# Attention and two feed-forward stages on one core: the turned one-hot evicted by VectorE, parameter blocks in odd steps, dummies among similarities, two casts moved

## The chip, the core and the metric

The kernel runs on one core of a Trainium2 chip. The metric is the device time of one execution in microseconds (us). Before the change the median of three runs is 686.15 us (684.75 to 687.68).

## What is computed

Clustered attention (two batches, 8 heads, 768 tokens, 64 per head), then a feed-forward stage behind a low-rank mixing over tokens, then one with a convolution over tokens and a gate. The change concerns the attention alone:

```python
q_assign = np.argmax(np.einsum('bhsd,hcd->bhsc', q_n, c_n), axis=-1)
k_assign = np.argmax(np.einsum('bhsd,hcd->bhsc', k_n, c_n), axis=-1)
mask = q_assign[:, :, :, None] == k_assign[:, :, None, :]
scores = scale * np.matmul(q, k.transpose(0, 1, 3, 2))
scores = np.where(mask, scores, -1000000000.0)
...
attn = attn / (np.sum(attn, axis=-1, keepdims=True) + 1e-09)
return np.matmul(attn, v).astype(np.float32)
```

## The kernel before

Heads are taken in pairs: 2 batches x 4 pairs, numbered 0 to 7 here. A pair has 12 **steps**, one for each tile of 128 queries of its two heads; 96 steps in all, numbered n, and s is the number of the step in its pair (0 to 11). Python code issues the instructions in the order in which each engine executes them; nothing is rearranged later. The function `step(n)` (L644) issues parts of several tiles:

- TensorE: the scores of tile n + 2 (`s_mm`, L344 from the split operands "ab", L355 from "cd", whose last rows hold the one-hot of the clusters and so the mask), products with v for three finished tiles (`pv_mm`, L406), every third step the turning of the output (`fin_t`, L422), and the transposes of tile n (`t_mm`, L382, two PSUM tiles of three transposes each).
- ScalarE: the rounded half of the transposes of tile n - 1 (`t_hi`, L391), the exponential of tile n + 1 (L373), in steps with s = 0, 3, 6, 9 the copy of the finished product (`fin_a`, L415), in steps 1, 4, 7, 10 that of the turned output (`fin_x`, L428).
- VectorE: the rest of the transposes of tile n - 1 (`t_lo`, L395, which needs L391), and the row maximum of tile n + 2 (`s_max`, L361), written out together with the scaled scores.

The transposes, similarities, turned outputs and turned one-hots share three PSUM tiles (pool `ps_t`, tag "t"): TensorE waits where none of the three has been emptied.

`prep(n)` (L613) issues at the end of a step what the next pair needs. The similarities with the centroids (`sims`, L220, 24 narrow matmuls) run in step 2. VectorE makes a one-hot of them in steps 2 to 5 (L239 to L247), TensorE turns it in step 6 (`onehot_t`, L253), ScalarE evicts it (`onehot_rows`, L259), and SP's queue copies it into "cd" (L267). In pair 0 all of this is one to two steps earlier. POOL splits the next operands (`split_ops`, L130 and L131, issued in steps 1 and 7; `split_v`, L122 and L123, in step 8) and issues their loads (L111 to L113, steps 3 and 10).

The weights arrive as 64-bit numbers and are converted in **parameter blocks**. Seven of them lie under the attention, one behind the other, one a pair: `pump(THIN)` takes the next action of a block at every second step (L642). Before, these are the even steps: DMA in step 2, conversion of the high word on ScalarE (`job_base`, L460) in step 6, the shift of the low word on VectorE (`job_low`, L465) in step 8, the joining of the words (`job_high`, L469) in step 10, the sign (`job_sign`, L473) in step 0 of the next pair, and in step 2 `job_put`: a cast on ScalarE (L519, or L547 for blocks of V; the first block, U, has none) and a subtraction on POOL (L520). From pair 4 on the mixing of batch 0 is issued in steps 0, 8, 9 and 11 as well (L566 to L605), with an addition of 512 columns on VectorE for each tile (L585).

At the start, `first_pair` prepares head 0 on its own; `split_first(1, "q")` (L203 to L205) rounds the second half of head 0's queries with two ScalarE casts and a POOL subtraction, and the loads and splits of head 1 follow on POOL. `warm` (L156) issues dummy matmuls of 384 columns on zeros, whose result is not used. The similarities of pair 1 run at the start too, tiles 0 and 1 before step -2 and tiles 2 to 5 in step 0.

Of the kernel before, what the change touches and what calls it, by code (L numbers as in the profile page):

```python
# [19 lines left out]
AF = mybir.ActivationFunctionType  # L20
ALU = mybir.AluOpType
# [10 lines left out]
def tile_kernel(ctx: ExitStack, tc: tile.TileContext, qk, vv, cen, u_w, v_w, w1, w2, win, wout, conv, out):  # L32
    nc = tc.nc
# [3 lines left out]
    NT = S // P  # L37
# [70 lines left out]
    def load_ops(b, p, j):  # L108
        h = 2 * p + j
        ab, cd = take_ops(b, p, j)  # L110
        nc.gpsimd.dma_start(out=cd[0:D], in_=qk[b, h])  # L111
        nc.gpsimd.dma_start(out=ab[D:2 * D], in_=qk[b, h])
        nc.gpsimd.dma_start(out=ab[0:D, 1 - j], in_=qk[b, h, :, 1 - j])  # L113
# [6 lines left out]
    def split_v(b, p, rv):  # L120
        vt = a_v.tile([P, 2, NT, 2 * D], F32R, tag="vt", name="vt")
        nc.gpsimd.tensor_copy(vt[:, :, :, 0:D], rv)  # L122
        nc.gpsimd.tensor_sub(vt[:, :, :, D:2 * D], rv, vt[:, :, :, 0:D])  # L123
        vts[b, p] = vt

    def split_ops(b, p, j, eng):

        ab, cd = ops[b, 2 * p + j]
        lo, hi = raw[b, p][j], raw[b, p][1 - j]
        eng.tensor_sub(ab[0:D, j], lo[0:D], cd[0:D, j])  # L130
        eng.tensor_sub(ab[D:2 * D, 1 - j], hi[D:2 * D], ab[D:2 * D, 1 - j])  # L131
# [13 lines left out]
    ohs = acon.tile([2 * 2 * NC, 2], F32, name="ohs")  # L145
# [10 lines left out]
    def warm(count):  # L156
        for _ in range(count):
            nc.tensor.matmul(idle, busy[:, 0:P], busy, start=True, stop=True)
# [36 lines left out]
    def split_first(half, which):  # L195
        c = slice(half * HS, (half + 1) * HS)
        if which == "k":
            nc.scalar.copy(cd0[0:D, 1, c], rk0[D:2 * D, c])
            nc.scalar.copy(ab0[0:D, 1, c], rk0[D:2 * D, c])
            nc.gpsimd.tensor_copy(ab0[D:2 * D, 1, c], rk0[D:2 * D, c])  # L200
            nc.vector.tensor_sub(ab0[D:2 * D, 1, c], rk0[D:2 * D, c], ab0[D:2 * D, 1, c])
        else:
            nc.scalar.copy(cd0[0:D, 0, c], rq0[0:D, c])  # L203
            nc.scalar.copy(ab0[D:2 * D, 0, c], rq0[0:D, c])
            nc.gpsimd.tensor_sub(ab0[0:D, 0, c], rq0[0:D, c], cd0[0:D, 0, c])  # L205
# [7 lines left out]
    def sims(b, p, tiles=range(NT)):  # L213
        rq, rk = raw[b, p]
        if (b, p) not in ohst:
            ohst[b, p] = {"pm": ps_t.tile([P, NT * 4, NC], F32, tag="t", name="sim")}
        pm = ohst[b, p]["pm"]
        for t in tiles:
            for i, (r, cb) in enumerate(((rq, cbq), (rk, cbk))):
                nc.tensor.matmul(  # L220
                    pm[:, 4 * t + 2 * i:4 * t + 2 * i + 2, :].rearrange("p g c -> p (g c)"),
                    r[:, t * P:(t + 1) * P], cb[:, p], start=True, stop=True,
                )
# [32 lines left out]
    def onehot_rows(b, p):  # L256
        pt = ohst.pop((b, p))["pt"]
        os_ = a_oh.tile([4 * NC, S], F32R, tag="os", name="os")
        nc.scalar.activation(os_, pt, AF.Identity, scale=ohs[:, 0:1], bias=ohs[:, 1:2])  # L259
        put_rows(b, p, os_, range(2))  # L260

    def put_rows(b, p, os_, heads):
# [104 lines left out]
    def s_exp(n):  # L367
        ps = st.pop(("s", n))
        nb = st.pop(("nb", n))
        if n % 3 == 0:  # L370
            st["sum", n // 3] = a_s.tile([P, 3], F32, tag="sum", name="sum")
        e = st["e", n]
        nc.scalar.activation(e, ps[:, :, 0:HS], AF.Exp, scale=SCALE, bias=nb, accum_out=st["sum", n // 3][:, n % 3:n % 3 + 1])  # L373
# [154 lines left out]
    load_ops(0, 0, 1)  # L528
    rv0 = load_v(0, 0)
    first_pair()  # L530
    split_first(1, "q")
    load_ops(0, 1, 0)
    sims(0, 1, range(2))
    split_ops(0, 0, 1, nc.gpsimd)
    split_v(0, 0, rv0)


    u3 = mixc.tile([P, NT, 3, R], F32, name="u3")
# [74 lines left out]
    def prep(n):  # L613

        pair, s = divmod(n, 2 * NT)
        nxt = pair + 1
        if nxt < B * NP:
            b, p = divmod(nxt, NP)
            for part, at in enumerate((2, 2, 3, 4, 5) if nxt > 1 else (0, 0, 1, 2, 3)):
                if s == at and (nxt > 1 or part > 1):  # L620
                    sims_onehot(b, p, part)
            if s == 1:
                split_ops(b, p, 0, nc.gpsimd)
            elif s == 3:
                load_ops(b, p, 1)
            elif s == 4:
                st["rv"] = load_v(b, p)
            elif s == 7:
                split_ops(b, p, 1, nc.gpsimd)
            elif s == 8:  # L630
                split_v(b, p, st.pop("rv"))
            if s == (6 if nxt > 1 else 5):
                onehot_t(b, p)
                onehot_rows(b, p)
        if s == 10 and pair + 2 < B * NP:
            load_raw(*divmod(pair + 2, NP))
            load_ops(*divmod(pair + 2, NP), 0)
        if n == NQ - 7:
            queue_chunk(1, lambda: wpc)
        if n >= NQ - 7:  # L640
            pump(FLOW)
        elif n % 2 == 0 and n > 0:  # L642
            pump(THIN)

    def step(n):
        pair, s = divmod(n, 2 * NT)
        mix = None
        if s == 8 and pair > 0 and n < NQ:
            b, p = divmod(pair - 1, NP)
            mixing.insert(0, mix_t(b, p))  # L650
            if p == NP - 1:
                mix_rest(b)
        if n == 0:
            sims(0, 1, range(2, NT))
        if n + 2 < NQ:
            s_mm(n + 2)
        g, r = divmod(n - 4, 3)
        if 0 <= g < NHALF:
            pv_mm(g, r)
        if 0 <= g - 1 < NHALF and r == 0:  # L660
            fin_t(g - 1)
        elif mixing and (s in (0, 8, 9, 11) or pair == B * NP - 1):
            mix = mixing.pop(0)
            got = mix[0]()
        if s == 2 and n < NQ and 1 < pair + 1 < B * NP:
            sims(*divmod(pair + 1, NP))
        if 0 <= n < NQ:
            t_mm(n)
        if 0 <= n - 1 < NQ:
            for i in range(2):  # L670
                t_hi(n - 1, i)
                t_lo(n - 1, i)
        if 0 <= n + 1 < NQ:
            s_exp(n + 1)
        if n == 0:
            sims_onehot(0, 1, 0)
            sims_onehot(0, 1, 1)
        if n + 2 < NQ:
            s_max(n + 2)
        if 0 <= g < NHALF and r == 0:  # L680
            sm = st["sum", g]
            nc.gpsimd.tensor_scalar(out=sm, in0=sm, scalar1=1e-9, scalar2=None, op0=ALU.add)
        if 0 <= g < NHALF and r == 2:
            fin_a(g)
        if 0 <= g - 1 < NHALF and r == 0:
            fin_x(g - 1)
        if mix:
            mix[1](got)
        if 0 <= n < NQ:
            prep(n)  # L690

    for n in range(-2, NQ - 2):
        step(n)
# [254 lines left out]
```

## Time and profile before

| | |
|---|---|
| median of three runs | 686.15 us |
| profiled execution, its own time | 687.84 us |
| its span | 685.9 us |
| TensorE busy (matmul) | 666.7 us, 97% |
| VectorE busy | 451.3 us, 66% |
| ScalarE busy | 373.1 us, 54% |
| POOL busy | 292.0 us, 43% |
| mean granted TensorE clock | 0.997 |

Attention takes the first 270 us of the span, up to its last exponential. The shares are averages over the stages: under attention VectorE and ScalarE are busy for 80 to 90% of the time, in the feed-forward stages for much less. Matmuls are pipelined and the ends of their rows are modelled, so TensorE's rate is better read from the starts of its matmuls. In a row of the timeline the engines are PE (TensorE), DVE (VectorE), ACT (ScalarE), POOL (GpSimd) and SPq (SyncE's queue); what stands in brackets is the idle time of the engine before the instruction and what ended it.

### The profile page before, as it was taken

The page shows a single profiled execution, that of the slowest core. Times are in us where ns is not written, and L with a number is a line of the kernel's source. Part 1 is how long each engine was busy: PE and PEld are TensorE (multiplying, and loading weights), DVE is VectorE, ACT ScalarE, POOL GpSimd, SP SyncE. Part 2 cuts the span into 40 slices and gives each one's busy share as a digit, 9 for nine tenths or more (in the row PEclk, how much of TensorE's full clock was granted, in tenths as well). Part 3 has the DMA queues.
Part 4 walks back from the last instruction along what each step waited for, and adds up shares of the span by engine and source line. Part 5 has one row for each costly group of instructions (what it writes and reads, how often), then busy time and mean ns, then how long its engine had stood idle before and what let it go on. Part 6 is the DMA issues. An engine that isn't in the chain of part 4 may idle for free.

```text
span 685.9 us, 10453 instructions
## 1 busy us (share of the span) xinstructions
PE 666.7 (97%) x3782; PEld 586.1 (85%) x3782; DVE 451.3 (66%) x833; ACT 373.1 (54%) x750; POOL 292.0 (43%) x384
## 2 busy tenths in 40 slices
PE   8999999998999999998999999999999999999997
PEld 6899999998899998888888888888887788888886
DVE  6897888888888898668732778775247535543400
ACT  5787787887787898324311443442134357753611
POOL 5775757585657542424530333332024643322300
PEclk9999999999999999999999999999999999999999
DMA  7764545546353501212200444342013000000111
GB/s 181 159 147 78 136 105 123 127 102 146 81 144 86 129 1 32 93 32 93 93 32 3 135 134 127 124 147 70 1 48 133 4 0 1 1 32 16 47 46 47
DMA packets 19587, 55.49 MB, mean 81 GB/s; under 512 B 3312, under 2 KB 7024, under 8 KB 19536
## 3 DMA queue, kind: packets, MB, share of 16 engines
q1 hardware_dynamic: 15936, 40.08, 19.5%
q0 software_dynamic: 3600, 14.75, 10.6%
q8 instruction: 30, 0.49, 0.3%
q14 instruction: 21, 0.17, 0.1%
HBM read 50.19 MB, written 3.15 MB: 78 GB/s over the span
## 4 chain that ended last, share of the span: by engine, by line
PE 78%; DVE 9%; issue 4%; ACT 4%; POOL 3%; DMA 0%; ACTq 0%; POOLq 0%; DVEq 0%
PE g L837 10%; PE tr L382 8%; PE pv L406 7%; PE h L714 5%; PE h L716 5%; PE h L715 5%; PE a L731 5%; PE a L730 5%; PE a L732 5%; PE sc L344 3%; PE sc L355 3%; PE po L871 3%; PE po L872 3%; PE po L873 3%; PE sim L220 2%
## 5 line engine op out<-in xcount | busy, mean ns | idle before, releaser
L520 POOL TENSOR_TENSOR wl<-wx,wh 128x512 fp32r<-128x512 f32 x48 | 63.0, 1314 | 114.9 <-ACT wh L519 114.6
L395 DVE TENSOR_TENSOR pl<-tr,ph 128x384 fp32r<-128x384 f32 x192 | 97.6, 549 | 17.7 <-ACT ph L391 16.9
L391 ACT CAST ph<-tr 128x384 fp32r<-128x384 f32 x192 | 83.8, 485 | 26.4 <-PE tr L382 25.6
L382 PE MATMUL tr<-identf,e 128*128 128x128 f32 x576 | 84.0, 278 | 10.1 <-DVE pl L395 7.5
L361 DVE TENSOR_SCALAR_CACHE_REDUCE e<-sc 128x768 f32<-128x768 f32 x96 | 90.8, 947 | 1.1 <-PE sc L355 1.1
L719 ACT ACTIVATE rh<-h 128x512 fp32r<-128x512 f32 (+1 forms) x52 | 29.3, 563 | 111.8 <-PE h L716 111.8
L373 ACT ACTIVATE e<-sc,nb 128x768 f32<-128x768 f32 x96 | 88.2, 918 | 3.1 <-DVE e L361 3.0
L720 DVE SCALAR_TENSOR_TENSOR rl<-h,rh 128x512 fp32r<-128x512 f32 (+1 forms) x52 | 33.7, 648 | 82.9 <-ACT rh L719 82.8
L382 PEld LDWEIGHTS tr<-identf,e 128*128 128x128 f32 x576 | 66.8, 142 | 19.7 <-DVE pl L395 14.3
L714 PE MATMUL h<-uh,wh 128*128 128x512 f32 (+1 forms) x208 | 78.2, 376 | 1.6 <-DVE rl L720 1.6
L730 PE MATMUL a<-rh,wh 128*128 128x512 f32 (+1 forms) x208 | 78.2, 376 | 0.5 <-DVE xa L746 0.5
L731 PE MATMUL a<-rl,wh 128*128 128x512 f32 (+1 forms) x208 | 77.9, 374 | 0.5 <-DVE rl L720 0.3
L716 PE MATMUL h<-uh,wl 128*128 128x512 f32 (+1 forms) x208 | 77.7, 373 | 0.0
L715 PE MATMUL h<-ul,wh 128*128 128x512 f32 (+1 forms) x208 | 77.7, 373 | 0.0
L732 PE MATMUL a<-rh,wl 128*128 128x512 f32 (+1 forms) x208 | 77.6, 373 | 0.0
L406 PE MATMUL pv<-ph,vt 128*128 128x384 f32 x192 | 65.7, 342 | 0.2 <-ACT asb L415 0.2
L406 PE MATMUL pv<-pl,vt 128*128 128x384 f32 x192 | 64.9, 338 | 0.0
L519 ACT CAST wh<-wx 128x512 fp32r<-128x512 f32 x48 | 29.8, 620 | 58.2 <-DVE wx L473 58.1
L344 PE MATMUL sc<-ab 128*128 128x384 f32 x192 | 57.8, 383 | 0.7 <-ACT e L373 0.3
L432 POOL TENSOR_TENSOR ats<-ats 128x192 f32<-128x192 f32 x32 | 19.6, 611 | 90.4 <-ACT ats L428 85.2
L854 POOL TENSOR_TENSOR h<-h,cv 128x768 f32<-128x768 f32 x16 | 29.6, 1851 | 64.5 <-ACT cv L853 64.5
L469 DVE SCALAR_TENSOR_TENSOR wx<-wb,wx 128x512 int32<-128x512 int32 (+3 forms) x52 | 49.0, 942 | 11.4 <-ACT wb L460 9.5
(137 smaller groups left out, 1523.3 us busy)
## 6 DMA issues: line engine op xcount, KB each, us to landing
raw<-in_w_dram SPq DMA_DIRECT2D x32, 512.0 KB, 3.7
cd<-in_qk_dram POOLq DMA_DIRECT2D x15, 384.0 KB, 4.3
ab<-in_qk_dram POOLq DMA_DIRECT2D x15, 384.0 KB, 5.4
raw<-in_win_dram SPq DMA_DIRECT2D x8, 512.0 KB, 3.6
raw<-in_wout_dram SPq DMA_DIRECT2D x8, 512.0 KB, 3.7
rv<-in_vv_dram SPq DMA_DIRECT2D x8, 384.0 KB, 3.0
out_dram<-o SPq DMA_DIRECT2D x24, 128.0 KB, 1.8
ab<-in_qk_dram POOLq DMA_DIRECT2D x15, 192.0 KB, 5.7
```

The lines of the kernel that those rows point to most:

```text
L361: nc.vector.tensor_scalar(out=e, in0=ps[:, :, 0:HS], scalar1=-SCALE, scalar2=3e38, op0=ALU.mult, op1=ALU.min, accum_out=nb,)
L373: nc.scalar.activation(e, ps[:, :, 0:HS], AF.Exp, scale=SCALE, bias=nb, accum_out=st["sum", n // 3][:, n % 3:n % 3 + 1])
L382: nc.tensor.transpose(pt[:, k, :], e[:, i, k * P:(k + 1) * P], identf)
L391: nc.scalar.copy(st["pt", n // 3][0][:, i * NK:(i + 1) * NK, n % 3, :], st["t", n, i])
L395: nc.vector.tensor_sub(lo, st.pop(("t", n, i)), hi)
L406: nc.tensor.matmul(acc, vt[:, h % 2, k, :], m[:, k].rearrange("p a b -> p (a b)"), start=(k == 0 and i == 0), stop=(k == NT - 1 and i == 1),)
L714: nc.tensor.matmul(ph, wh[:, k, ws], uh[g][:, k, ts], start=(k == 0), stop=False)
L715: nc.tensor.matmul(ph, wh[:, k, ws], ul[g][:, k, ts], start=False, stop=False)
L716: nc.tensor.matmul(ph, wl[:, k, ws], uh[g][:, k, ts], start=False, stop=(k == ND - 1))
L730: nc.tensor.matmul(accs[d][:, 0:n], wh[:, i, ds_], rh, start=(f == 0), stop=False)
L731: nc.tensor.matmul(accs[d][:, 0:n], wh[:, i, ds_], rl, start=False, stop=False)
L732: nc.tensor.matmul(accs[d][:, 0:n], wl[:, i, ds_], rh, start=False, stop=(f == NH - 1))
```

## The change

Four edits:

1. `onehot_rows` evicts the turned one-hot with a VectorE instruction in place of one of ScalarE (seven times, pairs 0 to 6).
2. `pump(THIN)` acts in odd steps from step 3 of pair 0 on, so every action of a block comes one step later: conversion in step 7, shift in step 9, joining in step 11, sign in step 1, cast in step 3.
3. In step 0 a dummy matmul follows the similarities of each of the tiles 2 to 5.
4. The second half of the first query split, and with it the loads and splits of head 1 on POOL, moves from before step -2 into step -1, behind the first exponential.

```diff
--- before.py
+++ after.py
@@ -256,7 +256,7 @@
     def onehot_rows(b, p):
         pt = ohst.pop((b, p))["pt"]
         os_ = a_oh.tile([4 * NC, S], F32R, tag="os", name="os")
-        nc.scalar.activation(os_, pt, AF.Identity, scale=ohs[:, 0:1], bias=ohs[:, 1:2])
+        nc.vector.tensor_scalar(out=os_, in0=pt, scalar1=ohs[:, 0:1], scalar2=ohs[:, 1:2], op0=ALU.mult, op1=ALU.add)
         put_rows(b, p, os_, range(2))
 
     def put_rows(b, p, os_, heads):
@@ -528,11 +528,7 @@
     load_ops(0, 0, 1)
     rv0 = load_v(0, 0)
     first_pair()
-    split_first(1, "q")
-    load_ops(0, 1, 0)
     sims(0, 1, range(2))
-    split_ops(0, 0, 1, nc.gpsimd)
-    split_v(0, 0, rv0)
 
 
     u3 = mixc.tile([P, NT, 3, R], F32, name="u3")
@@ -639,7 +635,7 @@
             queue_chunk(1, lambda: wpc)
         if n >= NQ - 7:
             pump(FLOW)
-        elif n % 2 == 0 and n > 0:
+        elif n % 2 == 1 and n > 1:
             pump(THIN)
 
     def step(n):
@@ -651,7 +647,10 @@
             if p == NP - 1:
                 mix_rest(b)
         if n == 0:
-            sims(0, 1, range(2, NT))
+
+            for t in range(2, NT):
+                sims(0, 1, (t,))
+                warm(1)
         if n + 2 < NQ:
             s_mm(n + 2)
         g, r = divmod(n - 4, 3)
@@ -672,6 +671,11 @@
                 t_lo(n - 1, i)
         if 0 <= n + 1 < NQ:
             s_exp(n + 1)
+        if n == -1:
+            split_first(1, "q")
+            load_ops(0, 1, 0)
+            split_ops(0, 0, 1, nc.gpsimd)
+            split_v(0, 0, rv0)
         if n == 0:
             sims_onehot(0, 1, 0)
             sims_onehot(0, 1, 1)
```

ScalarE at the start. Before:

```order
L307 ACTIVATE cd<-oht 16x384
L309 CAST cd<-oht 16x384
L203 CAST cd<-rq 64x384
L204 CAST ab<-rq 64x384
L373 ACTIVATE e,sum<-sc,nb 128x768 x2
L391 CAST ph<-tr 128x3x128 x2
L373 ACTIVATE e,sum<-sc,nb 128x768
L391 CAST ph<-tr 128x3x128 x2
```

With the change:

```order
L307 ACTIVATE cd<-oht 16x384
L309 CAST cd<-oht 16x384
L373 ACTIVATE e,sum<-sc,nb 128x768
L203 CAST cd<-rq 64x384
L204 CAST ab<-rq 64x384
L373 ACTIVATE e,sum<-sc,nb 128x768
L391 CAST ph<-tr 128x3x128 x2
L373 ACTIVATE e,sum<-sc,nb 128x768
```

The two casts (L203, L204) stand between the first and the second exponential instead of ahead of both.

VectorE in pair 2, from step 6 on ("wx" is the parameter block, "mt" the mixing, "os" the one-hot's rows). Before:

```order
L361 TENSOR_SCALAR e,nb<-sc 128x768
L395 TENSOR_TENSOR pl<-tr,ph 128x3x128 x2
L361 TENSOR_SCALAR e,nb<-sc 128x768
L431 RECIPROCAL rs<-sum 128x3
L395 TENSOR_TENSOR pl<-tr,ph 128x3x128 x2
L361 TENSOR_SCALAR e,nb<-sc 128x768
L574 TENSOR_TENSOR tt_297<-mt,tt_297 32x128
L465 TENSOR_SCALAR wx<-raw 96x384
L395 TENSOR_TENSOR pl<-tr,ph 128x3x128 x2
```

With the change:

```order
L361 TENSOR_SCALAR e,nb<-sc 128x768
L259 TENSOR_SCALAR os<-oht,ohs 64x768
L395 TENSOR_TENSOR pl<-tr,ph 128x3x128 x2
L361 TENSOR_SCALAR e,nb<-sc 128x768
L431 RECIPROCAL rs<-sum 128x3
L395 TENSOR_TENSOR pl<-tr,ph 128x3x128 x2
L361 TENSOR_SCALAR e,nb<-sc 128x768
L570 TENSOR_TENSOR tt_284<-mt,tt_284 32x128
L395 TENSOR_TENSOR pl<-tr,ph 128x3x128 x2
L361 TENSOR_SCALAR e,nb<-sc 128x768
L465 TENSOR_SCALAR wx<-raw 96x384
L395 TENSOR_TENSOR pl<-tr,ph 128x3x128 x2
```

The eviction (L259) stands behind the row maximum of step 6, and the shift (L465) one step later, behind the row maximum of step 9.

TensorE in step 7 of pair 1, behind the turned one-hot, with the engines whose semaphores are waited for ("at" is the turned output, "tr" the transposes). Before:

```order
L422 MATMUL at<-identf,asb 128x128 [waits Activation_49]
L422 MATMUL at<-identf,asb 128x128 x2
L382 MATMUL tr<-identf,e 128x128 [waits DVE_49]
L382 MATMUL tr<-identf,e 128x128 x2
L382 MATMUL tr<-identf,e 128x128 [waits DVE_49]
L382 MATMUL tr<-identf,e 128x128 x2
```

With the change:

```order
L422 MATMUL at<-identf,asb 128x128 [waits DVE_49]
L422 MATMUL at<-identf,asb 128x128 x2
L382 MATMUL tr<-identf,e 128x128 [waits DVE_49]
L382 MATMUL tr<-identf,e 128x128 x2
L382 MATMUL tr<-identf,e 128x128 [waits Activation_49]
L382 MATMUL tr<-identf,e 128x128 x2
```

The turned output now waits for VectorE, which empties the one-hot's PSUM tile. The second group of transposes waits for ScalarE: it gets the tile that the turned output has just used, where before it got one that VectorE empties.

## Rows read from the trace of the kernel before

**Rows 1.** Timeline, pair 3: start and length (us), engine, line, operation, tiles, [idle before]
```profile
116.33 0.52 ACT L547 CAST v<-wx 96x384 fp32r<-96x384 f32 x1
...
119.32 0.86 ACT L391 CAST ph<-tr 128x384 fp32r<-128x384 f32 x2 [2.47 <-PE tr L382]
...
119.36 0.59 PE L344 MATMUL sc<-ab 128*128 128x384 f32 x2
...
121.43 0.59 PE L344 MATMUL sc<-ab 128*128 128x384 f32 x2
```

**Rows 2.** Windows at the start: busy by engine, TensorE's granted clock, DMA share, GB/s
```profile
18.00:19.00 1.00, 1.00 (x7) 1.00 (x6) 0.83 (x1) 0.20 (x1) 1.00 (x1) 0.50 1.04 266
20.00:21.00 1.00, 1.00 (x9) 0.77 (x8) 1.00 (x2) 1.00 (x3) 1.00 (x1) 1.00 1.32 250
```

**Rows 3.** Timeline of the start, from the first pair's one-hot to head 1's splits
```profile
11.51 0.82 PE L158 MATMUL idle<-busy 128*128 128x384 bf16 x4
...
14.37 0.51 ACT L203 CAST cd<-rq 64x384 fp32r<-64x384 f32 x1
...
15.44 0.90 ACT L373 ACTIVATE e<-sc,nb 128x768 f32<-128x768 f32 x1
...
16.48 1.01 PE L344 MATMUL sc<-ab 128*128 128x384 f32 x2 [0.35 <-ACT e L373]
...
18.16 0.96 DVE L361 TENSOR_SCALAR_CACHE_REDUCE e<-sc 128x768 f32<-128x768 f32 x1 [0.85 <-PE sc L355]
...
20.43 0.95 DVE L361 TENSOR_SCALAR_CACHE_REDUCE e<-sc 128x768 f32<-128x768 f32 x1
...
22.42 1.83 POOL L123 TENSOR_TENSOR vt<-rv,vt 128x768 fp32r<-128x768 f32 x1
```

**Rows 4.** Timeline, pair 3, steps 6 and 7: the turned one-hot
```profile
127.63 0.95 DVE L361 TENSOR_SCALAR_CACHE_REDUCE e<-sc 128x768 f32<-128x768 f32 x1
...
128.68 0.99 ACT L259 ACTIVATE os<-oht,ohs 64x768 fp32r<-64x768 bf16 x1 [0.58 <-PE oht L253]
...
130.63 1.02 DVE L395 TENSOR_TENSOR pl<-tr,ph 128x384 fp32r<-128x384 f32 x2 [2.04 <-ACT ph L391]
...
131.24 1.01 PE L382 MATMUL tr<-identf,e 128*128 128x128 f32 x6 [0.66 <-DVE pl L395]
...
131.75 0.47 ACT L428 COPY ats<-at 128x384 f32<-128x384 f32 x1
```

**Rows 5.** Timeline, pair 2, steps 8 to 10; last row pair 5, step 8
```profile
102.43 0.59 PE L344 MATMUL sc<-ab 128*128 128x384 f32 x2
...
102.66 1.83 POOL L131 TENSOR_TENSOR ab<-rq,ab 64x768 fp32r<-64x768 f32 x1
...
102.67 2.03 DVE L465 TENSOR_SCALAR wx<-raw 96x384 int32<-96x384 int32 x1
...
105.47 1.84 POOL L123 TENSOR_TENSOR vt<-rv,vt 128x768 fp32r<-128x768 f32 x1
...
105.65 0.59 PE L344 MATMUL sc<-ab 128*128 128x384 f32 x2
...
202.87 0.43 DVE L465 TENSOR_SCALAR wx<-raw 128x512 int32<-128x512 int32 x1
```

**Rows 6.** Line 311, the first pair's eviction on VectorE: count, ns min/median/max, starts, shape
```profile
L311 DVE TENSOR_SCALAR os<-oht,ohs x2: 662/666/669, 12.0 to 13.2; 64x384 fp32r<-64x384 bf16 x2
```

**Rows 7.** Timeline, pair 4, step 11 to pair 5, step 1: an addition and a sign
```profile
178.58 0.59 PE L344 MATMUL sc<-ab 128*128 128x384 f32 x2
...
179.02 0.68 DVE L585 TENSOR_TENSOR x<-x,mu 128x512 f32<-128x512 f32 x1
...
179.62 0.68 DVE L473 SCALAR_TENSOR_TENSOR wx<-wb,wx 128x512 int32<-128x512 int32 x1
...
181.82 0.59 PE L344 MATMUL sc<-ab 128*128 128x384 f32 x2
```

## Prediction

> **What bounds the kernel now.** The change lies wholly in the attention stage, so I read, in this order: the granted clock at its start, the timeline there, one whole pair of heads in the timeline, and the groups of the edited lines. A step of attention in which nothing is added takes 2.07 us from one score matmul to the next (119.36 to 121.43) [rows 1]. That is TensorE's own work, so a step gets shorter only where it takes more than its matmuls need. It does at three kinds of place.
>
> *The start.* The granted clock is 0.50 of full (its 1.2 GHz level) at 18 us and 1.00 (2.4 GHz) again from 20 us [rows 2]. Before it fell, TensorE ran the narrow similarity matmuls and then stood 0.35 us until ScalarE had ended the first exponential (16.48) [rows 3].
>
> *Step 6 of a pair, the turned one-hot.* VectorE ends its row maximum at 128.58 and stands 2.04 us. ScalarE has idled 0.58 us for the turned one-hot, evicts it in 0.99 us and does a weight conversion, and only then comes the cast that VectorE's subtraction needs. TensorE then waits 0.66 us for a PSUM tile [rows 4].
>
> *Step 8, the parameter block.* The shift of a weight block (L465) takes 2.03 us if POOL has started a split 0.01 us before it, and 0.43 us where it came first (202.87) [rows 5]. Seven such shifts lie under attention. From the score matmul at 102.43 to the next at 105.65 are 3.22 us [rows 5], 1.15 over the 2.07. By the same reading pairs 1, 2 and 4 pay this, pairs 3, 5 and 6 do not.
>
> **The change, part by part.**
>
> *Start (casts and dummies).* Two casts of 0.51 us leave the front of the first exponential, which can then start when its row maximum is there, some 0.3 us before 15.44 [rows 3]. The four dummies cost TensorE 0.82 / 4 = 0.2 us each [rows 3], 0.8 together, before the third tile's scores. Those started at 16.48 and would start near 16.95, after the last dummy. At the full clock their two pairs of matmuls take some 0.85 us, so VectorE's third maximum comes near 17.95 instead of 18.16 [rows 3]. The second exponential is 1.0 us later than now (two casts); the first subtraction waits for the cast behind it, and the fourth maximum, now at 20.43 [rows 3], comes about 0.45 earlier.
>
> Against that, POOL's subtraction of the second cast's half, its three loads, both splits of head 1 and the split of v start about 1.7 us later. The last of them (22.42, 1.83 long) would end near 26.0 [rows 3], and the first product with v stands behind it; VectorE has work queued for the half microsecond that this may cost. But VectorE's one-hot steps between SBUF tiles now fall beside these splits and can be held as L465 is. I take 0.7 us for that. The sum is +0.3; if the clock falls all the same, the dummies run at half speed and the third maximum comes 0.6 later than now, so up to +1.5; with the clock held and no such hold, -0.5.
>
> *The eviction on VectorE, seven times.* No row has it. The nearest is the first pair's own: 0.66 us for half of the width [rows 6]. Twice that is 1.33; with the fixed part paid once it is 0.66 plus the 0.44 by which a maximum over 768 (0.95) exceeds a subtraction over 384 (1.02 / 2) [rows 4], so 1.10, which I take, since it has the same fixed part as the row; the upper end adds 7 x 0.23 = 1.6 us. ScalarE saves 0.99. So the work itself gets no cheaper; what counts is the order. The Trainium skill, "VectorE: DVE Perf Modes", section Specifications, says that ScalarE sits closer to PSUM and VectorE closer to SBUF. By it the eviction would be at its upper price, and the sum below would be 1.6 us higher.
>
> Replay of step 6 (pair 3) [rows 4]: maximum ends 128.58, eviction from 128.7 to 129.8, the subtraction starts there instead of at 130.63. The cast before it needs only the transposes and is done by then. TensorE's next transposes start near 130.6 instead of 131.24. Their second half, though, gets another PSUM tile than before (the order shows a wait for ScalarE where one for VectorE stood), the one that L428 empties; that comes behind an exponential and ends near 131.15. So 0.5 us is left of 0.83.
>
> But in pairs 2 to 6 the block's last cast moves from step 2 to step 3. In step 2 ScalarE stood 2.47 us beside the similarities, so the 0.52 us of such a cast (L547) cost nothing [rows 1]; in step 3 its casts follow one another, and VectorE, which works without a gap from there to step 6, gets its operand about 0.4 us later. I leave these pairs 0.25 us each. Pair 1 has no such cast: 0.5. Pair 0: 0.25. Together -0.25 - 0.5 - 5 x 0.25 = **-2.0**.
>
> *Odd steps.* The shift now comes at the end of step 9. POOL's queue, whose splits wait behind L428's and the reciprocal's results, is some 0.5 us earlier than before: the cast between its splits ends near 104.9 and L123 starts near 104.96 instead of 105.47 [rows 5]. VectorE would come to the shift near 104.73 in pair 2 and gets in between the two, as the held one did, which ended at 104.70. So pairs 1 and 2 get back 2 x 1.15, pair 0, whose block is narrower, 0.3 by estimate: **-2.6**. Pair 3 stays free.
>
> *Pairs 4 to 6.* Here batch 0's mixing adds a 0.68 us addition on VectorE in steps 9, 11 and 0 (L585), and the shift comes after it, well inside L123: held about 1.5 us, with no long matmuls beside it as in step 8. In step 11 addition and word (L469) now follow one another as addition and sign did in step 0 (179.02, 179.62) [rows 7]. There the score interval is 3.24 us (178.58 to 181.82) [rows 7], 0.85 over the 2.39 of a step with three more transposes. Counted so over steps 9 to 1, these pairs lose 2.7, 0.95 and 0.5 us before the change; held in step 10 and following VectorE's pace of 2.0 us plus additions until the next similarities, I get 2.2 us each: **+2.5**.
>
> Sum: 0.3 - 2.0 - 2.6 + 2.5 = -1.8. The profiled execution took 687.84 us, 1.69 above the median of 686.15; the sum applied to it gives 686.04, to the median 684.35, rounded to **684.4 us**. The later stages start earlier by what is won, and their order is unchanged.
>
> **Rivals.**
>
> *The one-hot step pays fully (faster).* If ScalarE makes up the moved cast in its idle spots and the shift is never held, six pairs win 0.5 each, pair 0 wins 0.25, the holds go, and pairs 4 to 6 stay as they are: 0.3 - 0.25 - 3.0 - 2.6 = -5.55, so 680.6 us. For it: VectorE's 2.04 us of standing is large [rows 4]. Against it: VectorE has no gap from step 3 to 6, and L585 comes ahead of the shift.
>
> *The shift meets L123 in every pair (slower).* My replay leaves 0.23 us between its arrival and L123's start; from the point where it arrives later, POOL's whole 1.84 us [rows 5] must pass. A hold of 1.6 us cost 1.15, so this costs about 1.4 in each of pairs 1 to 6, 8.4, against 4.0 now (1.15 twice, 1.4, 0.3). With +0.3 at the start, -2.0 for the one-hot and 0.6 for the crowded step 11: +3.3, so 689.5 us.
>
> *The dummies do not hold the clock.* Then the start costs +1.5 and the time is 685.6 us. For it: in rows 3 the clock fell although TensorE had little idle time. The Trainium skill, "TensorE: Matmul & The Clock Gate", section What's actually happening, says that the gate decides on a beat of its own that is not tied to the kernel's start; by that the dummies would help in some executions and not in others, and the time would lie between 684.4 and 685.6. One trace cannot show that.
>
> **How the numbers follow.** Forecast 0.50, with a range of its own of 682.5 to 686.5 from the start's and the eviction's bounds; one-hot pays fully 0.33; shift held everywhere 0.10; clock falls 0.07. A measurement of this kernel can tell about 0.5%, 3.4 us. Faster by more takes the first rival and a tail of 0.05 of the forecast: 0.38. Slower by more takes most of the second rival: 0.07. The rest, 0.55, is no change. The range of 80% runs from 680.0, a little under the first rival, to 688.0; what is left out is the second rival and the far tail of the first.
>
> **What would show it.** The granted clock stays 1.00 from 15 to 20 us. L259 is a VectorE row of 1.1 to 1.33 us, and the wait ahead of the subtraction in step 6 is gone. L465 in pairs 1 and 2 takes 0.4 to 0.9 us, in pairs 4 to 6 about 1.9. Wrong would be: score intervals around the one-hot that shrink by a full microsecond in all pairs, or shifts of 2 us in pairs 1 to 3.

## The result, and the profile after

The changed kernel takes 680.87 us at the median of 5 runs (680.56 to 682.5), the kernel before 687.58 beside it (684.75 to 689.41). The ratio is 0.9917, 95% interval 0.9888 to 0.9947: faster by 0.8%. The profiled execution took 682.39 us (before: 687.84). In both executions 416.7 to 416.8 us lie between the start of the last exponential and the end of the span, so all of the gain is in the attention, whose last exponential starts at 263.90 instead of 269.18.

The first section of the page after: of each engine the busy time, its share of the span and the number of instructions:

```profile
PE 664.6 (98%) x3786; PEld 585.1 (86%) x3786; DVE 454.9 (67%) x840; ACT 367.4 (54%) x743; POOL 292.7 (43%) x384
```

*The start.* Windows of the changed kernel, in the same columns as [rows 2]:

```profile
12.00:13.00 1.00, 1.00 (x4) 0.48 (x4) 0.60 (x2) 0.00 (x0) 0.00 (x0) 0.50 1.10 240
18.00:19.00 1.00, 1.00 (x9) 0.96 (x9) 0.97 (x3) 0.97 (x2) 0.97 (x2) 1.00 0.56 155
```

The granted clock is 1.00 at 18 us, where it was 0.50 before. But in this execution it was 0.50 (1.2 GHz) at 12 us, in the first scores and in the four dummies that follow them in both kernels, ahead of the place that the edits concern. It fell there at 10.70 us, behind 1.02 us in which TensorE stood. The timeline, which answers to [rows 3]:

```profile
10.34 0.35 PE L301 MATMUL oht<-identb,oh 128*64 128x128 bf16 x3 [1.02 <-DVE oh L247]
...
10.63 1.61 PE L344 MATMUL sc<-ab 128*128 128x384 f32 x4
...
12.04 1.50 PE L158 MATMUL idle<-busy 128*128 128x384 bf16 x4
...
16.07 0.33 PE L158 MATMUL idle<-busy 128*128 128x384 bf16 x1
...
16.55 0.90 ACT L373 ACTIVATE e<-sc,nb 128x768 f32<-128x768 f32 x1 [0.83 <-DVE e L361]
...
17.45 0.50 ACT L203 CAST cd<-rq 64x384 fp32r<-64x384 f32 x1
...
18.50 0.90 ACT L373 ACTIVATE e<-sc,nb 128x768 f32<-128x768 f32 x1
```

Four dummies took 1.50 us in place of 0.82, the first exponential came at 16.55 in place of 15.44, and waited for VectorE and not for a cast.

*Steps 6 and 7, pair 3*, timeline, against [rows 4]:

```profile
124.77 0.95 DVE L361 TENSOR_SCALAR_CACHE_REDUCE e<-sc 128x768 f32<-128x768 f32 x1
...
125.65 1.07 DVE L259 TENSOR_SCALAR os<-oht,ohs 64x768 fp32r<-64x768 bf16 x1
...
126.64 1.00 DVE L395 TENSOR_TENSOR pl<-tr,ph 128x384 fp32r<-128x384 f32 x2
...
127.49 0.48 ACT L428 COPY ats<-at 128x384 f32<-128x384 f32 x1 [0.68 <-PE at L422]
...
127.87 0.68 ACT L460 ACTIVATE wb<-raw 128x512 f32<-128x512 f32 x1
...
128.03 0.55 PE L382 MATMUL tr<-identf,e 128*128 128x128 f32 x3 [0.24 <-ACT ats L428]
128.05 0.59 POOL L432 TENSOR_TENSOR ats<-ats 128x192 f32<-128x192 f32 x1 [5.30 <-ACT ats L428]
...
128.33 0.59 PE L344 MATMUL sc<-ab 128*128 128x384 f32 x2
```

VectorE goes from the maximum to the eviction to the subtraction without a gap, where it stood 2.04 us. ScalarE has nothing to evict, and its weight conversion (L460) now follows L428 in step 7. Before, it stood between the eviction and the cast that VectorE waits for; these are the two rows behind the eviction of [rows 4]:

```profile
129.57 0.66 ACT L460 ACTIVATE wb<-raw 128x512 f32<-128x512 f32 x1
...
130.14 0.83 ACT L391 CAST ph<-tr 128x384 fp32r<-128x384 f32 x2
```

As predicted, the second half of the transposes waits for L428; it costs 0.24 us.

Below, an "interval of step s" is the time from the score matmul that step s issues (L344) to the next one. An instruction of VectorE is called held where it takes longer beside work of POOL than it does elsewhere. The interval of step 7 falls from 3.32 to 2.94 us in pairs 1 and 2 and from 3.43 to 2.94 in pairs 3 to 6.

*Steps 9 and 10, pair 2*, timeline, against [rows 5]:

```profile
102.57 0.59 PE L344 MATMUL sc<-ab 128*128 128x384 f32 x2
...
102.79 0.35 DVE L465 TENSOR_SCALAR wx<-raw 96x384 int32<-96x384 int32 x1
103.01 1.84 POOL L123 TENSOR_TENSOR vt<-rv,vt 128x768 fp32r<-128x768 f32 x1
...
104.95 0.59 PE L344 MATMUL sc<-ab 128*128 128x384 f32 x2
```

The shift comes 0.22 us ahead of POOL's subtraction and takes 0.35 us. (These rows are the interval of step 10; the shift is issued in step 9.) The interval of step 9, 3.22 us before, is 2.07 in pairs 1 to 3.

*The same place in pair 4*, where the mixing's addition (L581, in the kernel before L585) comes first:

```profile
165.30 0.68 DVE L581 TENSOR_TENSOR x<-x,mu 128x512 f32<-128x512 f32 x1
...
165.33 0.60 PE L344 MATMUL sc<-ab 128*128 128x384 f32 x2
165.50 1.84 POOL L123 TENSOR_TENSOR vt<-rv,vt 128x768 fp32r<-128x768 f32 x1
165.90 1.73 DVE L465 TENSOR_SCALAR wx<-raw 128x512 int32<-128x512 int32 x1
...
168.15 1.01 PE L382 MATMUL tr<-identf,e 128*128 128x128 f32 x6 [0.84 <-DVE pl L395]
...
168.91 0.59 PE L344 MATMUL sc<-ab 128*128 128x384 f32 x2
```

L123 has started 0.40 us before the shift, which takes 1.73 us; TensorE waits 0.84 us for what VectorE does next, and the interval of step 10 is 3.58 us where it was 2.40. Pairs 5 and 6 pay the same (3.64 and 3.41). What gives this back stands one sign later (pair 5, timeline, against [rows 7]):

```profile
173.79 0.59 PE L344 MATMUL sc<-ab 128*128 128x384 f32 x2
...
174.23 0.68 DVE L581 TENSOR_TENSOR x<-x,mu 128x512 f32<-128x512 f32 x1
...
176.19 0.59 PE L344 MATMUL sc<-ab 128*128 128x384 f32 x2
...
176.72 0.86 DVE L473 SCALAR_TENSOR_TENSOR wx<-wb,wx 128x512 int32<-128x512 int32 x1
```

The sign (L473) no longer follows the addition: that interval is 2.40 us in place of 3.24. The sign now falls into the next one, that of the similarities, which is 4.70 us long before and after, so there it costs nothing.

### The profile page after: what moved, and what is told of

Same layout as the page of the kernel before. It is cut to its first block, busy times and chain, and to the rows that moved or that the text cites. A ratio compares the mean times of both kernels' runs of the same rounds, so it can differ in the third digit from the quotient of the medians.

```text
span 680.6 us, 10458 instructions
## 1 busy us (share of the span) xinstructions
PE 664.6 (98%) x3786; PEld 585.1 (86%) x3786; DVE 454.9 (67%) x840; ACT 367.4 (54%) x743; POOL 292.7 (43%) x384
## 3 DMA queue, kind: packets, MB, share of 16 engines
q0 software_dynamic: 3600, 14.75, 10.7%
## 4 chain that ended last, share of the span: by engine, by line
PE 84%; DVE 7%; issue 4%; ACT 3%; POOL 2%; DMA 0%; ACTq 0%; POOLq 0%; DVEq 0%
PE g L841 10%; PE pv L406 9%; PE tr L382 8%; PE h L718 6%; PE h L720 5%; PE h L719 5%; PE a L735 5%; PE a L734 5%; PE a L736 5%; PE sc L344 4%; PE sc L355 4%; PE po L875 3%; PE po L876 3%; PE po L877 3%; PE sim L220 2%
## 5 line engine op out<-in xcount | busy, mean ns | idle before, releaser
L391 ACT CAST ph<-tr 128x384 fp32r<-128x384 f32 x192 | 83.8, 487 | 25.5 <-PE tr L382 24.4
L373 ACT ACTIVATE e<-sc,nb 128x768 f32<-128x768 f32 x96 | 88.4, 921 | 2.6 <-DVE e L361 1.5
L344 PE MATMUL sc<-ab 128*128 128x384 f32 x192 | 57.6, 382 | 0.3 <-ACT e L373 0.3
L469 DVE SCALAR_TENSOR_TENSOR wx<-wb,wx 128x512 int32<-128x512 int32 (+3 forms) x52 | 47.1, 905 | 11.4 <-ACT wb L460 9.4
L432 POOL TENSOR_TENSOR ats<-ats 128x192 f32<-128x192 f32 x32 | 20.6, 642 | 76.0 <-ACT ats L428 67.8
```

The lines of the kernel that those rows point to most:

```text
L344: nc.tensor.matmul(ps[:, f, 0:HS], ab[:, 0, c0:c0 + P], ab[:, 1, f * HS:(f + 1) * HS], start=True, stop=False)
```

## The experiments

To keep the start out of the comparison, one column of the table is the time from the first exponential of pair 1 to the last one (starts of the rows of L373 in each profiled execution). Profiles of the changed kernel and of two kernels that differ from it in the start alone agree in it within 0.04 us: the changed kernel 220.68, again 220.72, without dummies 220.69, casts ahead 220.68. The shift L465 is free at 0.35 us (96x384) or 0.42 us (128x512). That of pair 0 is narrower (128x192) and is held in all fourteen profiles, in the odd steps by POOL's other split (L131). The ratios are against the kernel before on the same chip.

| kernel | eviction | block in | median us | ratio, 95% interval | pair 1 to last exp | step 7, pairs 1 to 6 | L465 in pairs 0 to 6, us |
|---|---|---|---|---|---|---|---|
| before | ScalarE | even | 687.58 | 1 | 226.39 | 3.39 | 1.25 2.04 2.03 0.43 2.11 0.43 0.43 |
| e7 | VectorE | even | 685.28 | 0.9978 (0.9958 to 0.9998) | 224.80 | 2.94 | 1.25 1.48 1.48 1.55 1.55 1.55 1.55 |
| e2, with the start's edits | VectorE | even | 685.04 | 0.9905 (0.9884 to 0.9927) | 224.78 | 2.94 | 1.25 1.46 1.48 1.54 1.54 1.55 1.53 |
| e6 | ScalarE | odd | 680.58 | 0.9898 (0.9869 to 0.9927) | 218.77 | 2.87 | 1.08 0.91 0.90 0.96 0.42 0.42 1.80 |
| e1, with the start's edits | ScalarE | odd | 679.76 | 0.9830 (0.9804 to 0.9855) | 218.66 | 2.87 | 1.08 0.89 0.89 0.96 0.42 0.42 1.80 |
| changed | VectorE | odd | 680.87 | 0.9917 (0.9888 to 0.9947) | 220.68 | 2.94 | 1.09 0.35 0.35 0.43 1.73 1.76 1.26 |

The kernel before itself moved: its medians beside these kernels were 687.58, 692.18 (e1 to e4, 11 runs), 686.40 (e5 to e8, 17 runs) and 687.09 (e9 to e12, 11 runs). Ratios across these groups are therefore not compared; times and intervals are.

### One edit undone: e1 to e4

**e1, eviction by ScalarE again:**

```diff
-        nc.vector.tensor_scalar(out=os_, in0=pt, scalar1=ohs[:, 0:1], scalar2=ohs[:, 1:2], op0=ALU.mult, op1=ALU.add)
+        nc.scalar.activation(os_, pt, AF.Identity, scale=ohs[:, 0:1], bias=ohs[:, 1:2])
```

> The changed kernel with the eviction of the turned one-hot back on ScalarE. Theory A (the gain lies at the one-hot and at the shifts): in the profile the score interval of step 7 is 2.94 us in six pairs against 3.32 to 3.43 before, so 2.5 to 3.5 us come back in all, median 683.5 to 684.5, and the 2 us wait of VectorE ahead of the subtraction in step 6 is there again. Theory B (the gain lies at the start, dummies and casts): within 1 us of the changed kernel's 680.9.

679.76 us (679.67 to 680.46): 1.1 less than the changed kernel, where theory A had 2.5 to 3.5 more. The eviction on VectorE is not what gained. Step 7 is even shorter without it, and the shift is no longer held in pairs 4 and 5. The timeline of e1 in pair 4, where the changed kernel's shift comes behind L123:

```profile
164.20 0.82 POOL L122 CAST vt<-rv 128x768 fp32r<-128x768 f32 x1
...
164.36 0.60 PE L344 MATMUL sc<-ab 128*128 128x384 f32 x2
164.93 0.42 DVE L465 TENSOR_SCALAR wx<-raw 128x512 int32<-128x512 int32 x1
165.10 1.94 POOL L123 TENSOR_TENSOR vt<-rv,vt 128x768 fp32r<-128x768 f32 x1
```

The shift comes 0.57 us after the score matmul in both kernels. POOL's subtraction comes 0.74 us after it here and 0.17 us after it in the changed kernel. POOL's queue starts on L428's result, and ScalarE gets to L428 earlier where it evicts nothing: POOL's next instruction (L432) in step 7 of pair 3 starts 0.28 us ahead of the following score matmul in the changed kernel (128.05, 128.33) and 0.30 us behind it with ScalarE's eviction (e6 below: 127.77, 127.47). So the faster one-hot step brings POOL in front of the shift.

**e2, parameter blocks in even steps again:**

```diff
-        elif n % 2 == 1 and n > 1:
+        elif n % 2 == 0 and n > 0:
             pump(THIN)
```

> The changed kernel with the parameter blocks back in even steps. Theory A: the shift stands in step 8 again beside POOL's split and is held there in two or more of pairs 1 to 6, 1.15 to 1.45 us each, and the sign follows the mixing's addition in step 0 (0.85 us in pairs 5 and 6), while the holds of pairs 4 to 6 in step 9 (1.2 us each) go: 1 to 3 us slower, 682 to 684. Theory B: within 1 us of 680.9.

685.04 us (684.88 to 685.89): 4.2 more than the changed kernel, theory A's mechanism with a larger size (it had 1 to 3). All seven shifts are held, step 9's interval is 2.65 to 2.72 us in pairs 1 to 3 and 3.18 to 3.19 in pairs 4 to 6, and the sign meets the addition again (3.24).

**e3, without the dummies:**

```diff
-            for t in range(2, NT):
-                sims(0, 1, (t,))
-                warm(1)
+            sims(0, 1, range(2, NT))
```

> The changed kernel without the four dummies among pair 1's similarities. Theory A: the first exponentials come some 0.4 us earlier if the clock stays up and the median stays within 0.7 us of 680.9. Theory B: without the dummies the clock falls behind the similarities in most executions and the median is 1.2 us or more above 680.9.

680.79 us (680.75 to 682.59), as theory A had it. Three runs of five have a mean granted clock of 0.999 or 1.0 and take 680.75 to 680.79; two have 0.994 and 0.995 and take 682.59 and 682.39. The profiled one is of the latter, and its windows show the clock low in two places:

```profile
12.00:13.00 1.00, 1.00 (x4) 0.47 (x4) 0.63 (x2) 0.00 (x0) 0.00 (x0) 0.50 1.16 240
18.00:19.00 1.00, 1.00 (x4) 0.98 (x4) 0.75 (x2) 0.97 (x2) 0.95 (x1) 0.50 0.35 72
```

**e4, the two casts and POOL's work ahead again:**

```diff
+    split_first(1, "q")
+    load_ops(0, 1, 0)
     sims(0, 1, range(2))
+    split_ops(0, 0, 1, nc.gpsimd)
+    split_v(0, 0, rv0)
...
-        if n == -1:
-            split_first(1, "q")
-            load_ops(0, 1, 0)
-            split_ops(0, 0, 1, nc.gpsimd)
-            split_v(0, 0, rv0)
```

> The changed kernel with the two casts, and the loads and splits of head 1 behind them, back ahead of the first exponential. Theory A: POOL's splits are 1.7 us earlier again, VectorE's one-hot steps in pair 0 are held less (0.94 and 0.90 us in the changed kernel, 0.35 and 0.82 before) and the median is 0 to 1 us lower, 680 to 681. Theory B: 0.5 us or more above 680.9.

680.81 us (680.62 to 681.79), the changed kernel's time. The first exponential comes at 15.41, against 14.92 in the changed kernel at the full clock (e9); at the first of pair 1 (41.66 against 41.56) only 0.1 us of the 0.5 is left. Theory A's reason did not come: with POOL's splits ahead again L243 is held longer in pair 0 (1.28 us against 0.94).

### One edit alone: e5 to e7

**e5, the kernel before, unaltered:**

> The unchanged kernel, for its profile on another chip, where it took 692.2 us at the median against 687.6 in the comparison with the changed kernel. Theory: its time hangs on a tie, since POOL's split and VectorE's shift reach their start in step 8 within 0.01 us of each other; where VectorE loses the tie the shift takes 2.0 us. If so, a profile of 690 us or more shows the shift held in five or six of the seven pairs (before: three), and the score intervals of steps 8 to 9 there at 3.2 us; one near 686 shows three or four. Rival: the chip's data path or DMA is slower, then all stages are longer by the same share and the number of held shifts is as before.

One run, 688.74 us. The timeline in pairs 1 and 5, step 8:

```profile
71.44 0.36 DVE L465 TENSOR_SCALAR wx<-raw 96x384 int32<-96x384 int32 x1
71.45 2.04 POOL L131 TENSOR_TENSOR ab<-rq,ab 64x768 fp32r<-64x768 f32 x1
...
201.94 1.84 POOL L131 TENSOR_TENSOR ab<-rq,ab 64x768 fp32r<-64x768 f32 x1
201.95 2.12 DVE L465 TENSOR_SCALAR wx<-raw 128x512 int32<-128x512 int32 x1
```

Here pair 1 is free and pair 5 held; in the execution of [rows 5] it was the other way round (2.04 and 0.43 us, table). Beside pair 0, pairs 4 and 5 are held, fewer than a time near 690 was expected to show: the rest of this execution's time is at the start, where its clock stayed at 0.50 from 16 to 22 us and pair 1's first exponential came at 44.40 instead of 42.79. So it is shown that at a distance of 0.01 us the one that starts first goes free, and that this falls differently in two executions of the kernel, on two occasions; why the median beside e1 to e4 lies at 692 is not settled.

**e6, odd steps alone**, the kernel before with this edit:

```diff
-        elif n % 2 == 0 and n > 0:
+        elif n % 2 == 1 and n > 1:
             pump(THIN)
```

> The kernel before with nothing but the odd steps. Theory 'odd steps carry all': within 1.5 us of the changed kernel, 679.5 to 682.5 us; shifts in pairs 1 to 3 of 0.3 to 1.0 us, step 7's score interval near 2.9 us although ScalarE evicts the one-hot, because the weight conversion no longer stands between that eviction and the cast that VectorE waits for. Rival 'the eviction carries a good part' (the prediction's terms): 684 us or more, step 7's interval at 3.3 us as before.

680.58 us (679.55 to 681.73): the changed kernel's time with one edit of four. The six runs are in two groups, 679.55 to 679.90 and 681.25 to 681.73, and the median lies between them; the profiled one is of the lower. The upper one is not explained. Pair 3, steps 6 and 7:

```profile
124.71 0.99 ACT L259 ACTIVATE os<-oht,ohs 64x768 fp32r<-64x768 bf16 x1 [0.57 <-PE oht L253]
...
125.60 0.83 ACT L391 CAST ph<-tr 128x384 fp32r<-128x384 f32 x2
...
126.09 1.02 DVE L395 TENSOR_TENSOR pl<-tr,ph 128x384 fp32r<-128x384 f32 x2 [1.16 <-ACT ph L391]
...
127.47 0.59 PE L344 MATMUL sc<-ab 128*128 128x384 f32 x2
127.58 0.68 ACT L460 ACTIVATE wb<-raw 128x512 f32<-128x512 f32 x1
127.77 0.59 POOL L432 TENSOR_TENSOR ats<-ats 128x192 f32<-128x192 f32 x1 [5.81 <-ACT ats L428]
```

The cast (L391) follows the eviction at once, since the conversion has moved to step 7. VectorE still stands 1.16 us, but 0.88 less than before, and that is enough: step 7 takes 2.87 us.

**e7, the eviction alone**, the kernel before with the VectorE line of e1's diff in place of the ScalarE line.

> The kernel before with nothing but the eviction on VectorE. Theory 'either edit empties step 6': step 7's score interval falls from 3.3 to 2.9 us in pairs 1 to 6, 2.5 to 3 us in all, but the shifts of step 8 stay where they were against POOL's split, held in three or more pairs; so 2 to 4 us less than the kernel before on the same chip, and no less if more shifts are held, since VectorE then comes later to them. Rival 'the eviction costs VectorE as much as it saves': within 1 us of the kernel before, step 7's interval 3.2 to 3.4 us.

685.28 us (684.94 to 686.92); the ratio's interval ends at 0.9998, so a gain of 0.2% is just told from none. Step 7 falls to 2.94 us here too, but the shifts pay for it (pair 2, step 8):

```profile
99.89 1.84 POOL L131 TENSOR_TENSOR ab<-rq,ab 64x768 fp32r<-64x768 f32 x1
...
100.47 1.48 DVE L465 TENSOR_SCALAR wx<-raw 96x384 int32<-96x384 int32 x1
```

L131 starts 0.58 us ahead of the shift and not 0.01: the same lead that POOL gets in e1's comparison. The tie is gone, and VectorE loses in every pair. Both theories were half right.

### Moving POOL's split of v: e8, e10 to e12, with e9 as their base

(e8 itself ran on the chip of e5 to e7, e9 on that of e10 to e12.)

**e8, split of v in step 11 in place of step 8:**

```diff
-            elif s == 8:
-                split_v(b, p, st.pop("rv"))
...
+        if s == 11 and nxt < B * NP:
+            split_v(*divmod(nxt, NP), st.pop("rv"))
```

> The changed kernel with the split of v issued in step 11 in place of step 8. Theory 'the held shift of pairs 4 to 6 costs 1.2 us each': the shifts take 0.4 us in all seven pairs, step 10's interval in pairs 4 to 6 falls from 3.5 to 2.4 us, 677 us or some 3.5 less than the changed kernel. Rival: the split, 2.8 us of POOL, now stands ahead of the next pair's first operands split in step 1 and holds the addition (step 0) or the sign (step 1), or it lets the product with v wait: intervals of steps 0 to 3 grow by 0.5 to 1 us in each pair, and the time stays at 680 to 682.

679.58 us (679.47 to 679.73), 219.48 in the table's measure. Both theories hold in part. The shifts of pairs 4 to 6 are free, and step 10 there takes 2.39, 2.39 and 2.56 us (3.3 less in all). But the joining of step 11 now stands beside the split (timeline, pairs 2 and 6):

```profile
105.97 1.22 DVE L469 SCALAR_TENSOR_TENSOR wx<-wb,wx 96x384 int32<-96x384 int32 x1
...
106.85 1.03 POOL L122 CAST vt<-rv 128x768 fp32r<-128x768 f32 x1
...
234.71 1.85 POOL L123 TENSOR_TENSOR vt<-rv,vt 128x768 fp32r<-128x768 f32 x1
235.66 1.45 DVE L469 SCALAR_TENSOR_TENSOR wx<-wb,wx 128x512 int32<-128x512 int32 x1
```

In the changed kernel the joining took 0.55 us in pair 2 and 0.68 in pair 6. In pair 6 it lies inside L123. In pair 2 the row of L122 begins only after the joining would have ended undisturbed (106.52), so there the edit shows the cause and the rows do not show how. The interval of the next pair's step 0 grows by 0.16 to 0.44 us in five pairs and by 0.77 in the last, 2.1 in all, which leaves 1.2.

**e9, the changed kernel, unaltered:**

> The changed kernel unaltered, on the chip of the next three, as their base: 680 to 683 us, with the spread coming from TensorE's granted clock at the start alone (about 1.7 us for a stretch at 0.50), and shifts held in pairs 4 to 6 only.

680.86 us (680.8 to 681.6); one run of six has a clock of 0.997 and it is the 681.6. Ratio 0.9912 (0.9893 to 0.9932).

**e10, e8 and e1 together** (both diffs):

> The changed kernel with the one-hot evicted by ScalarE again and the split of v issued in step 11. With ScalarE's eviction the shift is held in pair 6 alone (1.8 us, 1.5 us of score interval). Theory 'the holds add up by place': that hold goes, step 11's joining is 0.7 us longer in every pair beside the split's cast, which gives 0.3 us in each of five pairs and 0.8 in the last: sum near 0, so 679 to 680.5 us, like either edit alone. Rival: VectorE has more room in step 11 when it doesn't evict, the joining is hidden, 677.5 to 678.5 us.

680.09 us (679.93 to 681.7): the sum by place holds. The shifts of pairs 1 to 6 are free, pair 6's joining takes 1.45 us, and the two edits that each won about 1.2 us win 0.8 together, since with ScalarE's eviction only one shift was held.

**e11, split of v in step 10** (e8 with 10 for 11).

> The changed kernel with the split of v issued in step 10, behind the output's normalisation and ahead of the loads. Theory: the shift of step 9 is free in all pairs (0.35 to 0.43 us), but the 1.84 us subtraction now starts where VectorE comes to the joining of step 11, which is held for up to 1.5 us in pairs 1 to 3 (score interval of step 0 near 3 us in place of 2.06) and meets it later in pairs 4 to 6: 680 to 683 us, nothing won. Rival: VectorE gets in first in step 11, then 677 to 678 us.

682.45 us (682.12 to 684.12). The shifts of pairs 1 to 6 are free, but the joining is held in pairs 4 to 6, not in pairs 1 to 3 as expected, and step 4 of pairs 1, 3 and 4 is 0.5 to 0.7 us longer, for the reason that e12 shows (L243 takes 1.18, 1.39 and 1.52 us there). Pair 4, timeline:

```profile
171.67 1.84 POOL L123 TENSOR_TENSOR vt<-rv,vt 128x768 fp32r<-128x768 f32 x1
172.09 1.97 DVE L469 SCALAR_TENSOR_TENSOR wx<-wb,wx 128x512 int32<-128x512 int32 x1
```

**e12, split of v in step 1 of its own pair:**

```diff
+        if s == 1 and pair > 0:
+            split_v(*divmod(pair, NP), st.pop("rv"))
```

> The changed kernel with the split of v issued in step 1 of its own pair, ahead of the first operands' splits. Theory: shifts and joinings of steps 9 and 11 are free in all pairs (0.35 to 0.69 us), 3.5 us won there; the operands' splits move 2.7 us later and meet the one-hot's instructions of steps 2 to 5 between SBUF tiles, which gives back 0 to 0.5 us a pair: 677 to 680 us. Rival: the one-hot becomes late for step 6, or the product with v waits for its operand in step 4, then 682 us or more.

682.17 us (682.02 to 682.33). Joinings are free in all pairs and shifts in pairs 1 to 6, and the hold has moved to the one-hot (pair 3, step 4), where an instruction that took 0.35 us before meets the later split of the operands:

```profile
117.59 1.84 POOL L131 TENSOR_TENSOR ab<-rk,ab 64x768 fp32r<-64x768 f32 x1
...
118.27 1.38 DVE L243 TENSOR_TENSOR eq<-eq,iota 128x384 bf16<-128x384 bf16 x1
```

Step 4's interval is 2.86 to 3.27 us in pairs 1 to 6, where the changed kernel has 2.38 to 2.48. The expected 0 to 0.5 us a pair was too little.

No version beats the others clearly. e8 has the lowest median, 1.3 us (0.2%) under the changed kernel, though on another occasion, and its trace shows where; e1 and the lower group of e6 do nearly as much with fewer edits.

## Why the prediction was right or wrong

The time lay in the range (680.0 to 688.0) but under the forecast (684.4) and under its own range (682.5 to 686.5). The likeliest class, no change by the 0.5% that the prediction took as measurable, did not come: the gain is 0.8%. The first rival, "the one-hot step pays fully", gave 680.6, close to 680.87, and its terms came near: 0.38 to 0.49 us in six pairs, the holds of pairs 1 and 2 gone, pairs 4 to 6 unchanged in sum. But that the number fits is in part luck. It wanted the shift never held, and pairs 4 to 6 stay as they are only because their new holds cost what the freed signs and the old hold give; and it too booked the one-hot's gain to the eviction.

*Start, +0.3.* Inside its bounds (-0.5 to +1.5), but not at its value. The score matmul of pair 0's step 6 starts at 29.97 us in the profile of the kernel before, at 29.65 in the changed kernel at the full clock (e9) and at 31.30 in its profiled execution, whose clock fell at 10.70: -0.3 and +1.3. The edits of the start alone are worth less: 29.75 and 29.76 with them (e1, e2), 29.79 and 29.85 without (e6, e7). The term that was mis-sized is the dummies: in e9 the similarities of a tile follow each other every 0.53 us with a dummy, 0.45 without one in the kernel before, so a dummy cost 0.08 us and not 0.2. The first exponential comes at 14.92 (e9), 0.52 before [rows 3]; of that 0.1 us reaches pair 1 (e4). L243 was held in pair 1's one-hot (0.94 us, against 0.35 in the kernel before), but this does not hang on POOL's later splits alone: it took 1.28 us in e4, where they are ahead, and 0.74 in e5. The first product with v waited 0.50 us for L123.

The third rival, that the dummies do not hold the clock, did not come at its place. In none of the nine profiled executions with dummies did the clock fall between 14 and 23 us; in all five without them it fell between 15.9 and 17.6 us. e3, which has the casts moved and no dummies, is among the five, and e4, which has the dummies and not the casts, among the nine, so the profiles, one execution of each kernel, speak for the dummies. It does not fall in every run without them: three of e3's five have a mean clock of 0.999 or 1.0. Over all runs, means of 0.998 or less occur in 9 of 48 of the kernels with dummies, in 24 of 39 of the kernel before, in 15 of 18 of e6 and e7. With dummies it can still fall ahead of them, as in the changed kernel's profile (10.70 us) and in e11's (8.93). Such a fall cost 1.6 and 1.0 us at the score matmul named above (31.30 and 30.62); one at 16.2 to 17.0 us cost 0.3 or less (29.97, 29.79, 29.85). So the dummies guard mostly against a small loss; a longer fall in the same place, as in e5 (16 to 22 us), cost more (31.55). The prediction named a rule of the Trainium skill there, "TensorE: Matmul & The Clock Gate", section What's actually happening: the gate decides on a beat of its own that does not start with the kernel. That executions of one kernel differ agrees with it (two of five runs of the changed kernel at 0.997, three at 0.999 or 1.0); the beat itself no run shows.

*Eviction on VectorE, -2.0.* The price was right: 1.07 us seven times (1064 to 1069 ns), not 1.33, against 0.99 on ScalarE. The Trainium skill puts ScalarE closer to PSUM ("VectorE: DVE Perf Modes", section Specifications). The rows agree in sign, by 8%; the upper price that the prediction set beside that sentence did not come, and the sum was rightly made without it. The intervals gained more than forecast: 0.38 in pairs 1 and 2, 0.49 in pairs 3 to 6 (2.7 us), and 0.73 in pair 0's step 6 (2.82 to 2.09). The step that failed is the 0.25 us that the moved cast of step 3 was to give back in pairs 2 to 6: step 3's interval stays at 2.07, and only step 4 of pairs 4 to 6 is longer, by 0.09. The second failure is larger: the term was booked to the eviction. e6 shows that the odd steps alone give it, because they take the conversion L460 out from between eviction and cast. The prediction named that conversion in its rows and never asked what its moving alone would do. On top of the odd steps the eviction costs 2.0 us from pair 1 on (220.68 against 218.66), and pair 0 gives 0.85 back (first exponential of pair 1: 41.56 in e9 against 42.41 in e1).

*Odd steps, -2.6.* Right where it was worked out: the shift keeps 0.22 us ahead of L123 (0.23 foretold), and pairs 1 and 2 gain 1.15 each. Pair 0 gains 0.4 in steps 9 to 11 (7.20 to 6.76), though its shift stays held at 1.09 us. The second rival, the shift held in every pair, did not come; e2 and e7 show it, with even steps.

*Pairs 4 to 6, +2.5.* The mechanism was right, the shift inside L123 with 1.73 us. So was the state after, 2.2 us a pair, within 0.4: over steps 9 to 1 the intervals lose 2.17, 2.20 and 2.63 us against undisturbed ones (2.07, 2.39, 2.07, 2.07, 2.40 from pairs 1 to 3). The step that failed is the count before, "2.7, 0.95 and 0.5": by the same counting it was 3.49, 1.66 and 1.82. The sign's collision with the addition of [rows 7] recurs in the next two pairs (3.22 and 2.91 us against 2.40); that accounts for 1.3 of the 2.8 us by which the count was short, and for the rest the prediction shows no working. So the term is 0.0 in place of +2.5.

Together these three, 2.5 us here, 1.4 of the eviction's term and 0.6 of the start's, are most of the 5.2 us between the 686.04 that the sum gave for the profiled execution and the 680.82 of e9's. The forecast itself was only 3.5 us off, because it took the sum from the median of three runs, 1.7 us lower.

## What to carry to other kernels

Two edits of one change may empty the same gap: before booking a gain to an edit, replay the place with each edit alone, and ask of every instruction between the late result and its producer whether it could be elsewhere. Where a change crowds a stretch, count the stretch before by the same rule in every repetition, not in the one that was read. And where two engines hold each other, an improvement anywhere upstream shifts who comes first: compare arrival times against the nearest common event (here the score matmul), since 0.2 to 0.6 us decided 1.2.

## What was unexpected of the hardware

Which VectorE instructions POOL holds follows their operands, as far as these rows go. L465, L469 and L243 read only SBUF tiles and are held: 0.35 to 2.04 us, 0.55 to 1.22 and 0.35 to 1.38, each for tiles of one shape. The addition L581, one of whose operands is in PSUM, took 0.68 us beside L123 as well as without. The eviction from PSUM always took 1.07, but no instruction of POOL ran beside it in the changed kernel, so it says nothing on this. The Trainium skill says, in "SBUF — State Buffer", section Who interferes with whom: VectorE shares a pair of ports with GpSimd, and instructions with two inputs in SBUF (beside a GpSimd instruction that reads SBUF), or in a two-port mode, contend for it. The rows agree for L469 and L243, which have two inputs in SBUF, and for the addition; L465 has one input, and no row names its mode. They show the other direction too: L131 took 2.04 us in place of 1.84 where the shift, 0.36 long, was first (e5).

The time of the kernel before spread over 9 us (684.75 to 694.06 in 44 runs on four occasions), that of the changed kernel over 2 (680.56 to 682.5 in 11 runs on two). The tie is one cause; how much of the 9 us is its share is not shown. And TensorE's clock fell in some executions of a kernel and not in others: at 10.7 us behind 1.02 us of standing (the changed kernel, e3), at 8.93 us behind narrow similarity matmuls with no idle time before (e11), and at 15.9 to 17.6 us behind narrow similarity matmuls where no dummies stand among them.
